# Gate weights and bias through TensorE, another chunk order, split first tile, uneven sums: one change to a fused attention and MLP kernel

## The chip, the cores and the metric

The kernel runs on one core of a Trainium2 chip. The metric is the device time of one execution in microseconds, as the median of several runs. A profile of one execution comes with each kernel. Its "span" goes from the first to the last recorded instruction, so it is about 2 us shorter than the time. Engines are named as in the profile: PE is TensorE's matmuls, PEld its weight loads, DVE is VectorE, ACT is ScalarE, POOL is GpSimd, SP is SyncE, which issues most DMAs (SPq). "L318" is line 318 of the kernel in question. The change shifts line numbers by up to a dozen, so the same instruction has two numbers in the two kernels.

## The reference, cut to what matters

```python
# x: [1, 2048, 448]   16 heads of 28   bf16
q, k, v = split(x @ wqkv)                       # per head
pq, pk  = q @ w_phi, k @ w_phi                  # a 28x28 map per head
phi     = concat(softmax(p), softmax(-p))       # for q and k
kv, z   = sum_s phi_k[s] v[s]^T, sum_s phi_k[s]
o       = (phi_q @ kv) / (phi_q @ z + 1e-6)
a       = o @ wo
b       = gelu(x @ w1 + b1) @ w2 + b2
g       = sigmoid((x * gate_w).sum(-1))
out     = g * a + (1 - g) * b
```

The kernel folds the map into the projections: `Wpk = Wk · map` and `Wpq = Wq · map` are computed once on TensorE (the w_ps products), and then `x @ Wpk` gives `pk` directly. The gate `x · gate_w` is had for nothing as a 449th column of the V or Q projection, and for that the 448 gate weights must stand as a column beside the weights. `b1` must likewise stand as columns, one value per partition, to be the bias of the gelu.

## The kernel before

The order of work in the front part on TensorE is: transposes of the first 512 rows of x (`turn`), V products of the first two units, the Wk map products, K0, the Wq map products, then K1 and V2 (the first V unit with the gate column), and from there a dense run of projections. A unit is two tiles of 128 rows. Cuts are marked by `# ...`.

```python
    nc.gpsimd.dma_start(gb[16:19, :], gate_w[0:384].rearrange("(c p) -> c p", p=P))
    # ... the rest of gate_w and b1 into other rows of gb
    nc.gpsimd.dma_start(b2b[:], B_b2[None, :].to_broadcast([P, D]))

    load_wT(WkT, D)                               # DMA transposes on SP, in this order
    load_wT(WqT, 0)
    load_x(512, 512)
    nc.sync.dma_start_transpose(gbT[:], gb[:])    # rows of gb become columns
    load_x(1024, 512)

    def prep(W_T, W_out, s, copies):              # W_out = W * map, 4 chunks of 128 rows
        for h in (1, 0):
            w_ps = pair("w_ps", slot=(s + 1 - h) % 4)
            for i in range(2):
                c = 2 * h + i
                for m in range(4):
                    # ... one product, 84 to 168 columns
            copies[1 - h](out=W_out[:, 2 * h:2 * h + 2, 0:D], in_=w_ps[:, :, 0:D])

    turn(0, 1, nc.scalar.copy)                    # 4 transposes, one copy
    turn(2, 2, nc.vector.tensor_copy)
    idle(1)                                       # a filler matmul
    v0a = V(0, 3)
    # ... V products
    prep(WkT, Wpk, 1, (nc.scalar.copy, nc.vector.tensor_copy))
    # ... K0
    prep(WqT, Wpq, 3, (nc.vector.tensor_copy, nc.vector.tensor_copy))
    nc.vector.tensor_copy(out=Wpq[:, :, D], in_=gbT[:, 16:20])
    nc.vector.tensor_copy(out=WvG[:, :, D], in_=gbT[:, 16:20])
    nc.vector.tensor_copy(out=b1T[:], in_=gbT[:, 0:NJ])
    # ...
    visit([(K, 1), (V, 2)], [(Q, 0)], 0, 2)
```

PSUM is handled as four slots of two banks each. V2 takes slot 3, the slot in which chunks 2 and 3 of Wpq were summed, so it must wait until these have been copied out. In the middle of the MLP, the eight pairs of heads are summed into kv (`kv_half(0)`, `kv_half(1)`), each half is multiplied by a mask on VectorE, and the first four output tiles are computed from it (`nm` products, then a chain on VectorE that ends in `o_all`).

The softmax here doesn't subtract the row's maximum and nothing guards it: scores larger than these inputs give would overflow.

## Time and profile before

| what | value |
|---|---|
| time, median of 3 runs | 152.53 us (152.49 to 152.59) |
| span of the profiled run | 150.3 us |
| TensorE busy | 144.6 us, 96% of the span |
| VectorE, ACT, POOL busy | 81.7, 63.9, 73.4 us |
| TensorE's longest wait after the start | 1.24 us before V2 |

TensorE is idle for 5.7 us of the span. 3.1 us of that come after its last product, when only the last results have to be added up and stored. The other 2.6 us come before V2 starts, and they are most of what a change that doesn't alter the work can win back. The prediction shows the lines of the chain of waits and of TensorE's timeline.

### The profile page before, as it was taken

What the parts mean: (1) busy time and instruction counts of PE and PEld (TensorE: products, weight loads), DVE (VectorE), ACT (ScalarE), POOL (GpSimd) and SP (SyncE); (2) the same over time, 40 slices, a digit from 0 to 9 for tenths busy, and PEclk for the clock granted to TensorE, in tenths of its full rate; (3) what the DMA queues carried; (4) which work ended last, traced back from release to release, by engine and by line L of the source; (5) the groups of instructions that cost most, each with busy time, mean ns of one, the idle gap of its engine ahead of it and who ended that gap; (6) DMA issues with size and microseconds to landing.
All of it is one profiled execution on the core that took longest, in us unless ns stands there. A gap on an engine that the chain in (4) does not pass through costs nothing.

```text
span 150.3 us, 3083 instructions
## 1 busy us (share of the span) xinstructions
PE 144.6 (96%) x1281; PEld 74.2 (49%) x1281; DVE 81.7 (54%) x139; ACT 63.9 (43%) x71; POOL 73.4 (49%) x60
## 2 busy tenths in 40 slices
PE   7989799999999999999999999999999999999991
PEld 2445344555544444774444445554455555545561
DVE  0248488999969992049995000740637847044112
ACT  3346277989999876506767674000000000000000
POOL 7992127799996999900399960000611110024000
PEclk9999999999999999999999999999999999999999
DMA  4997969679999959994629991140302423303201
GB/s 88 290 196 120 209 153 191 136 170 220 218 219 231 361 126 138 212 120 96 74 41 173 173 139 36 37 100 10 122 31 65 100 70 70 70 2 120 65 31 31
DMA packets 46334, 18.99 MB, mean 126 GB/s; under 512 B 36784, under 2 KB 46128, under 8 KB 46320
## 3 DMA queue, kind: packets, MB, share of 16 engines
q1 hardware_dynamic: 45568, 18.18, 58.3%
q10 hardware_dynamic: 544, 0.37, 0.9%
q0 software_dynamic: 208, 0.23, 0.9%
q8 instruction: 10, 0.16, 0.5%
q14 instruction: 4, 0.03, 0.1%
HBM read 6.34 MB, written 1.84 MB: 54 GB/s over the span
## 4 chain that ended last, share of the span: by engine, by line
PE 88%; DMA 7%; SPq 1%; DVE 1%; issue 0%
PE hp L431 28%; PE y L526 28%; PE y L204 6%; PE q_ps L234 5%; DMA gel<-in_A_wqkv_dram 4%; PE k_ps L234 4%; DMA gbT<-gb 3%; PE v_ps L234 3%; PE nm L455 3%; PE kv L443 2%; PE v_ps L204 2%; PE q_ps L204 2%; PE k_ps L204 2%; PE y L214 1%; PE w_ps L315 1%; SPq L116 1%
## 5 line engine op out<-in xcount | busy, mean ns | idle before, releaser
L526 PE MATMUL y<-w_sb,gel 128*128 128x448 bf16 (+1 forms) x224 | 43.8, 350 | 0.0
L431 PE MATMUL hp<-xT,w_sb 64*128 64x512 bf16 x224 | 42.8, 376 | 0.0
L431 PE MATMUL hp<-xS,w_sb 64*128 64x512 bf16 x168 | 40.7, 376 | 0.0
L435 ACT ACTIVATE gel<-hp,b1T 128x1024 bf16<-128x1024 f32 x28 | 30.8, 1113 | 14.6 <-PE hp L431 14.2
L526 PEld LDWEIGHTS <-gel 128*128 128x128 bf16 x238 | 22.3, 98 | 19.3 <-issue 0.4
L431 PEld LDWEIGHTS <-w_sb 64*128 64x128 bf16 x392 | 18.9, 94 | 23.2 <-DVE o_all L468 0.5
L491 POOL TENSOR_SCALAR b2u<-b2b,ungate 128x448 f32<-128x448 bf16 x16 | 10.0, 637 | 40.5 <-DVE res L538 40.5
L261 POOL TENSOR_TENSOR gel<-gel,rec 128x1792 bf16<-128x1792 bf16 x8 | 25.6, 3212 | 7.1 <-DVE lg L270 4.8
L538 DVE SCALAR_TENSOR_TENSOR res<-y,ungate,b2u 128x448 bf16<-128x448 f32 (+1 forms) x16 | 10.3, 673 | 25.0 <-PE y L526 13.2
L261 POOL TENSOR_TENSOR phiq<-phiq,rec 128x1792 bf16<-128x1792 bf16 x4 | 12.7, 3211 | 9.6 <-DVE rec L260 9.6
L252 ACT ACTIVATE gel<-k_ps 128x896 bf16<-128x896 f32 x16 | 13.7, 922 | 6.5 <-PE k_ps L214 4.9
L258 DVE TENSOR_REDUCE sums<-gel 128x64 f32<-128x1792 bf16 x8 | 16.0, 1996 | 0.0
L462 DVE TENSOR_SCALAR den<-nm,enL 128x16 f32<-128x16 f32 x16 | 3.6, 228 | 17.2 <-PE nm L455 17.2
L261 POOL TENSOR_TENSOR phqT<-phqT,rec 128x1792 bf16<-128x1792 bf16 x4 | 12.7, 3213 | 0.0
L468 DVE TENSOR_TENSOR o_all<-nm,den 128x448 bf16<-128x448 f32 (+2 forms) x24 | 11.0, 485 | 0.6
L234 PEld LDWEIGHTS <-xT 64*128 64x128 bf16 x104 | 8.6, 94 | 4.8
L204 PEld LDWEIGHTS <-xT 128*128 128x128 bf16 x66 | 5.9, 98 | 8.1 <-issue 2.8
L280 DVE CAST vaug<-v_ps 128x896 bf16<-128x896 f32 x7 | 7.5, 1072 | 4.3 <-PE v_ps L214 2.9
L260 DVE RECIPROCAL rec<-sums 128x64 f32<-128x64 f32 x16 | 8.9, 553 | 1.1
L234 PEld LDWEIGHTS <-xS 64*128 64x128 bf16 x78 | 7.3, 94 | 3.6
L234 PE MATMUL q_ps<-gel,xT 64*128 64x448 bf16 x48 | 8.6, 349 | 0.0
L204 PE MATMUL y<-wo_sb,phiq 128*128 128x448 bf16 (+1 forms) x36 | 8.2, 349 | 0.0
(88 smaller groups left out, 149.5 us busy)
## 6 DMA issues: line engine op xcount, KB each, us to landing
w_sb<-in_B_w_dram SPq DMA_DIRECT2D x4, 784.0 KB, 12.3
out_dram<-res SPq DMA_DIRECT2D x15, 112.0 KB, 1.7
w_sb<-in_B_w_dram SPq DMA_DIRECT2D x1, 1568.0 KB, 16.6
xS<-xT SPq DMA_DIRECT2D x8, 96.0 KB, 2.2
phqT<-gel SPq DMA_DIRECT2D x4, 168.0 KB, 3.0
gel<-in_A_x_dram SPq DMA_DIRECT2D x2, 224.0 KB, 4.2
phqT<-gel SPq DMA_DIRECT2D x2, 168.4 KB, 3.2
gel<-in_A_wqkv_dram ACTq DMA_DIRECT2D x1, 336.0 KB, 4.3
```

The costliest lines, as they stand in the source:

```text
L204: nc.tensor.matmul(o, lhsT=self.L(i, slice(0, P), c), rhs=self.R(slice(0, P), c)[:, n0:n1], start=(first and c == 2), stop=(last and c == 1))
L234: nc.tensor.matmul(o, lhsT=tok, rhs=(W if direct else SWAPPED[name])[rows, c, 0:n], start=(k == 0), stop=own)
L252: nc.scalar.activation(out=o, in_=src, func=ACT.Exp, scale=(1.0, -1.0)[s])
L258: nc.vector.reduce_sum(out=sums[:], in_=ph, axis=AX.X)
L260: nc.vector.reciprocal(out=rec[:], in_=sums[:])
L261: eng.tensor_tensor(out=ph, in0=ph, in1=rec[:, :, :, None].to_broadcast([P, 32, 2, DH]), op=ALU.mult)
L431: nc.tensor.matmul(hp[:, i, :].rearrange("p (b t) -> p b t", b=2), lhsT=w1_sb[i * HP:(i + 1) * HP, k, j * P:(j + 1) * P], rhs=x_half(i, k, ...
L435: nc.scalar.activation(out=dst, in_=hp[:].rearrange("p i (b t) -> p i b t", b=2), func=ACT.Gelu_apprx_tanh, bias=b1T[:, j:j + 1])
L468: nc.vector.tensor_tensor(out=o_tok[:, col:col + (b - a) * DH].rearrange("p (q j d) -> p q j d", j=2, d=DH), in0=nm[:, a // 2:b // 2, 0:56 ...
L491: nc.gpsimd.tensor_scalar(out=b2u[t][:], in0=b2b[:], scalar1=ungate[:, place(t):place(t) + 1], scalar2=0.0, op0=ALU.mult, op1=ALU.add)
L526: nc.tensor.matmul(o, lhsT=gel[:, j, tok], rhs=w2_sb[:, j, n0:n1], start=(first and j == 0), stop=(last and j == NJ - 1))
L538: nc.vector.scalar_tensor_tensor(out=res[t][:, n0:n1], in0=o, scalar=ungate[:, e:e + 1], in1=b2u[t][:, n0:n1], op0=ALU.mult, op1=ALU.add)
```

## The change

Its intent: gate and b1 are turned into columns by two matmuls against the identity, with all 128 rows of the array (hence the zeroed 128x128 tiles gb and bb), in place of the DMA transpose. The chunks of the map products are computed in the order 2, 0, 3, 1, and the second Wpq copy goes to ACT. The first tile of x is transposed in two pairs, which VectorE and ACT copy out side by side, and the filler matmul goes. The second load of the map is issued by ACT rather than SP. The sums are cut six pairs and two pairs rather than four and four. The prediction counts these five parts in this order as parts 1 to 5. The broadcast of b2 moves from POOL to the end of SP's loads. The core of the diff, with cuts marked by `...`:

```diff
-    nc.sync.dma_start(wphi[0:HP, 3, :], wflat[384:448, :])
+    nc.scalar.dma_start(wphi[0:HP, 3, :], wflat[384:448, :])
...
-    nc.gpsimd.dma_start(b2b[:], B_b2[None, :].to_broadcast([P, D]))
...
     load_x(512, 512)
-    nc.sync.dma_start_transpose(gbT[:], gb[:])
     load_x(1024, 512)
...
+    def turned_rows(cols, rows):
+        nc.tensor.matmul(cols, lhsT=rows[:], rhs=ident[:, 0:cols.shape[-1]], start=False, stop=True,
+                         skip_group_check=True)
+
+    def prep(W_T, W_out, s, copies, gates=False):
+        w_ps = [pair("w_ps", slot=(s + 1 - h) % 4) for h in (1, 0)][::-1]
+        for c in (2, 0, 3, 1):
...
+            if c == 3 and gates:
+                cols = w_ps[1][:, 1, D:D + 4]
+                turned_rows(cols, gb)
+                for W in (WvG, Wpq):
+                    nc.vector.tensor_copy(out=W[:, :, D], in_=cols)
         for h in (1, 0):
-            copies[1 - h](out=W_out[:, 2 * h:2 * h + 2, 0:D], in_=w_ps[:, :, 0:D])
+            copies[1 - h](out=W_out[:, 2 * h:2 * h + 2, 0:D], in_=w_ps[h][:, :, 0:D])
...
-    turn(0, 1, nc.scalar.copy)
-    turn(2, 2, nc.vector.tensor_copy)
-    idle(1)
+    turn(0, 1, nc.vector.tensor_copy, 2, 4)
+    turn(0, 2, nc.scalar.copy, 0, 2)
+    turn(2, 0, nc.vector.tensor_copy)
...
-    prep(WqT, Wpq, 3, (nc.vector.tensor_copy, nc.vector.tensor_copy))
-    nc.vector.tensor_copy(out=Wpq[:, :, D], in_=gbT[:, 16:20])
-    nc.vector.tensor_copy(out=WvG[:, :, D], in_=gbT[:, 16:20])
-    nc.vector.tensor_copy(out=b1T[:], in_=gbT[:, 0:NJ])
+    prep(WqT, Wpq, 3, (nc.vector.tensor_copy, nc.scalar.copy), True)
...
+    nc.sync.dma_start(b2b[:], B_b2[None, :].to_broadcast([P, D]))
...
+            if kind is V and u == 3:
+                turned_rows(x_.un.ps[:, 1, 460:460 + NJ], bb)
...
-            kv_half(0)
-            kv_half(1)
+            parts = (range(0, 6), range(6, 8))
+            for qs in parts:
+                kv_part(qs)
```

More of the change, by code (lines that the diff above doesn't have):

```diff
@@ L97 @@
     hm = consts.tile([P, 4, 16], BF16, name="hm")
-    gb = consts.tile([32, P], BF16, name="gb")
-    gbT = consts.tile([P, 32], BF16, name="gbT")
+    gb = consts.tile([P, P], BF16, name="gb")
+    bb = consts.tile([P, P], BF16, name="bb")
     b1T = consts.tile([P, NJ], F32, name="b1T")
@@ L113 @@
     nc.vector.memset(gb[:], 0.0)
+    nc.vector.memset(bb[:], 0.0)
     xv = x[0:512, :].rearrange("(j p) d -> p j d", p=P)
@@ L153 @@
                             compare_op=ALU.is_ge, fill=0.0, base=DH - 1, channel_multiplier=-1)
-    nc.gpsimd.dma_start(gb[16:19, :], gate_w[0:384].rearrange("(c p) -> c p", p=P))
-    nc.gpsimd.dma_start(gb[19:20, :].rearrange("o (i p) -> o i p", i=2),
+    nc.gpsimd.dma_start(gb[0:3, :], gate_w[0:384].rearrange("(c p) -> c p", p=P))
+    nc.gpsimd.dma_start(gb[3:4, :].rearrange("o (i p) -> o i p", i=2),
                         gate_w[None, None, 384:448].to_broadcast([1, 2, HP]))
-    nc.gpsimd.dma_start(gb[0:NJ, :], B_b1.rearrange("(j p) -> j p", p=P))
     pk4 = phik.rearrange("p t (q m) -> p (t q) m", m=HP)
@@ L164 @@
     nc.gpsimd.memset(pq4[:, :, 56:64], 0.0)
+    nc.gpsimd.dma_start(bb[0:NJ, :], B_b1.rearrange("(j p) -> j p", p=P))
     nc.gpsimd.memset(o_all[:], 0.0)
@@ L283, in done @@
                 gate(u, t)
+            if u == 3:
+                nc.vector.tensor_copy(out=b1T[:], in_=t[:, 1, 460:460 + NJ])
     class K:
@@ L306, in twin @@
         nc.scalar.copy(out=W_T[:, :, D:512], in_=W_T[:, :, 384:D])
-    def prep(W_T, W_out, s, copies):
-        for h in (1, 0):
-            w_ps = pair("w_ps", slot=(s + 1 - h) % 4)
-            for i in range(2):
-                c = 2 * h + i
-                for m in range(4):
-                    n0, n1 = HEADS[m][0] * DH, HEADS[m][1] * DH
-                    nc.tensor.matmul(w_ps[:, i, n0:n1], lhsT=W_T[:, m, c * P:(c + 1) * P],
-                                     rhs=bd[:, m, 0:n1 - n0], start=(m == 0), stop=(m == 3),
-                                     skip_group_check=True)
-            copies[1 - h](out=W_out[:, 2 * h:2 * h + 2, 0:D], in_=w_ps[:, :, 0:D])
+    def turned_rows(cols, rows):
[4 more added lines that the diff above has]
+        for c in (2, 0, 3, 1):
+            h, i = c // 2, c % 2
+            for m in range(4):
+                n0, n1 = HEADS[m][0] * DH, HEADS[m][1] * DH
+                nc.tensor.matmul(w_ps[h][:, i, n0:n1], lhsT=W_T[:, m, c * P:(c + 1) * P],
+                                 rhs=bd[:, m, 0:n1 - n0], start=(m == 0), stop=(m == 3),
+                                 skip_group_check=True)
+            if c == 3 and gates:
[3 more added lines that the diff above has]
+                    nc.vector.tensor_copy(out=W[:, :, D], in_=cols)
+        for h in (1, 0):
+            copies[1 - h](out=W_out[:, 2 * h:2 * h + 2, 0:D], in_=w_ps[h][:, :, 0:D])
     def idle(n):
@@ L327, with turn @@
     idle(8)
-    def turn(j, slot, copy):
+    def turn(j, slot, copy, c0=0, c1=4):
         tp = pair("tp", BF16, slot)
-        for c in range(4):
+        for c in range(c0, c1):
             dlo = c * P if c < 3 else (384 if j < 2 else 320)
             nc.tensor.transpose(tp[:, 0, c * P:(c + 1) * P], x0[:, j, dlo:dlo + P], ident[:])
-        copy(out=xT[:, :, j * P:(j + 1) * P], in_=tp[:, 0, 0:512].rearrange("p (c t) -> p c t", c=4))
-    turn(0, 1, nc.scalar.copy)
-    turn(2, 2, nc.vector.tensor_copy)
-    idle(1)
+        copy(out=xT[:, c0:c1, j * P:(j + 1) * P],
+             in_=tp[:, 0, c0 * P:c1 * P].rearrange("p (c t) -> p c t", t=P))
+    turn(0, 1, nc.vector.tensor_copy, 2, 4)
+    turn(0, 2, nc.scalar.copy, 0, 2)
+    turn(2, 0, nc.vector.tensor_copy)
     v0a = V(0, 3)
@@ L436, in w1_unit, with kv_part @@
                              func=ACT.Gelu_apprx_tanh, bias=b1T[:, j:j + 1])
-    def kv_half(m):
+    def kv_part(qs):
         kv = pair("kv")[:, 0, :]
-        qs = range(4 * m, 4 * m + 4)
+        n = len(qs)
         for t in range(NT):
-            for q in qs:
-                nc.tensor.matmul(kv[:, (q % 4) * PW:(q % 4 + 1) * PW], lhsT=phik[:, t, q * P:(q + 1) * P],
-                                 rhs=vaug[:, t, q, :], start=(t == 0 and q == qs[0]),
+            for i, q in enumerate(qs):
+                nc.tensor.matmul(kv[:, i * PW:(i + 1) * PW], lhsT=phik[:, t, q * P:(q + 1) * P],
+                                 rhs=vaug[:, t, q, :], start=(t == 0 and i == 0),
                                  stop=(t == NT - 1), skip_group_check=True)
-        nc.vector.tensor_tensor(out=KVbd[:, 4 * m:4 * m + 4, :],
-                                in0=kv[:, 0:4 * PW].rearrange("p (q n) -> p q n", q=4),
-                                in1=mask[:, None, :].to_broadcast([P, 4, PW]), op=ALU.mult)
+        nc.vector.tensor_tensor(out=KVbd[:, qs[0]:qs[0] + n, :],
+                                in0=kv[:, 0:n * PW].rearrange("p (q n) -> p q n", q=n),
+                                in1=mask[:, None, :].to_broadcast([P, n, PW]), op=ALU.mult)
     def o_turned(t):
@@ L495 @@
         if j == 6:
-            kv_half(0)
-            kv_half(1)
+            parts = (range(0, 6), range(6, 8))
+            for qs in parts:
+                kv_part(qs)
             nms = [pair("nm"), pair("nm")]
             nms = [p[:, i, :] for p in nms for i in range(2)]
-            for m in range(2):
+            for qs in parts:
                 for t in range(4):
-                    num_mm(t, nms[t], range(4 * m, 4 * m + 4))
+                    num_mm(t, nms[t], qs)
             for t in range(4):
```

## The prediction

> **What bounds the kernel now.** I read the page first: TensorE is busy for 96% of the span, the granted clock is 0.9 or more in every slice, and the slices that are not full are at the front.
>
> ```profile
> PE 144.6 (96%) x1281; PEld 74.2 (49%) x1281; DVE 81.7 (54%) x139; ACT 63.9 (43%) x71; POOL 73.4 (49%) x60
> ...
> PE   7989799999999999999999999999999999999991
> ```
>
> So the time is TensorE's work plus TensorE's idle time, and a change that leaves the work alone can only win idle time. Second I listed TensorE's own waits, which are short:
>
> ```profile
> PE v_ps L204 <- DVE gel L367: 1.2, 1, 1.2
> PE w_warm L322 <- PEq L587: 0.8, 1, 0.8
> PE w_ps L315 <- DMA gel<-in_A_wqkv_dram: 0.3, 1, 0.3
> ```
>
> Third, the chain of waits in order of time (start us, us, what) says what stands behind the 1.2 us:
>
> ```profile
> 2.94 6.14 DMA gel<-in_A_wqkv_dram
> ...
> 9.13 0.41 PE w_ps L315 x4
> ...
> 9.57 0.88 PE w_ps L315 x12
> ...
> 10.48 0.46 DVE gel L318
> 10.94 4.68 DMA gbT<-gb
> ...
> 15.64 0.18 DVE gel L366
> 15.81 0.08 DVE gel L367
> ...
> 16.03 1.30 PE v_ps L204 x6
> ```
>
> The little transpose of gate and bias through the DMA queue takes 4.68 us from issue to landing; a VectorE copy then puts the gate column into WvG, and the V2 matmuls wait for it. From 16.03 to 61.57 the chain is TensorE alone. The timeline of TensorE (start, us) gives the front step by step:
>
> ```profile
> 4.50 1.03 PE L333 MATMUL tp<-ident,gel 128*128 128x128 bf16 x8
> 5.33 0.59 PE L322 MATMUL w_warm<-const-bfloat16-1.0 128*128 128x512 bf16 x1
> 5.79 0.74 PE L204 MATMUL v_ps<-gel,xT 128*128 128x448 bf16 x3
> 6.36 0.61 PE L333 MATMUL tp<-ident,gel 128*128 128x128 bf16 x8
> ```
>
> The later places with idle time are at the kv sums. In the chain the second half of the nm products begins at 65.81 though the first sixteen, 28.5 ns apart, were issued by 65.62: 0.19 us go on the second mask multiply (VectorE, 65.36 to 65.76). Then the fourth w1 unit after it loads its weights late, at 71.06 ("DVE o_all L468", 0.49 us on the weight loads), which makes the matmuls some 0.16 us late.
>
> **What the Trainium skill says.** (1) "DMA: Bandwidth & Descriptors", section "Issuing engines are not separate DMA queues": starting DMAs on a second engine saves only the sequencer's issue time. The trace has that time: the second map load occupies the SP queue for 0.565 us. (2) Same page, "Anatomy of one DMA — SWDGE (gpsimd) path": a fixed cost of about 2 us, measured on the gpsimd path, mostly the wait for the write receipt. The gbT transpose, issued from SP, has 4.68 us, over twice that; the trace decides. (3) "TensorE: Matmul & The Clock Gate", section "Wait — 56ns, not 53.3ns?": warm matmuls start every N / 2.4 GHz plus about 2.5 ns, so 189 ns for 448 columns; fourteen y matmuls take 2.65 us, 189 ns each, which agrees. (4) "VectorE: DVE Perf Modes", section "The TRN2 errata — SBUF-src ops pay a fixed extra latency per instruction": a copy out of PSUM costs 120 cycles at 0.96 GHz plus its columns. For 896 columns that is 1.06 us, and the trace has 1.09. I use its slope for the sizes that the trace lacks.
>
> **Part 1, gate and b1 by matmul.** It removes the DMA transpose (1.12 us of SP issue, 4.68 us of latency) and three VectorE copies of 0.17 us. It adds one 4-column and one 14-column matmul with 128-column weights, about 0.06 us each (the 84- to 168-column w_ps matmuls run at 0.93 / 16 = 0.058 us: 12.56 to 13.49), and three VectorE copies. The gate column is now made after twelve of the sixteen Wq products, so V2 no longer waits for a DMA. It waits instead for its PSUM slot: V2 takes slot 3, where chunks 2 and 3 of Wpq lie until VectorE has copied them out.
>
> **Part 2, chunk order 2, 0, 3, 1.** Chunk 3 needs the ACT copy of the last columns. Before, the Wk products stop after four (9.13) and go on at 9.57; four at 0.067 us would be 0.27, so about 0.17 us are lost. With chunk 0 in between, nothing is. The price is that ACT's copy of chunks 2 and 3 starts after twelve products, not eight, but the K0 products wait on VectorE's copy of chunks 0 and 1, which comes after all sixteen anyway. One Wpq copy goes to ACT, which in the old trace was idle for 3.18 us just there.
>
> **Part 3, the first x tile in two pairs.** The filler matmul goes and V0 can start after eight transposes, near 5.35: VectorE's 256-column copy should take 0.42 - 0.13 = 0.29 us (estimate, slope as in (4)) from about 4.95, ACT's about 0.4 (the 128x256 copy has 0.41) from 5.14 to 5.55. That would be 0.4 us, but the next transposes need the second x load, and its sixteenth landing event in the trace is at 6.00. Their weight loads began at 6.18, so only about 0.2 us is kept: the V products end at 8.60, not 8.80.
>
> **Part 4, half the map load on ACT.** The Wk transpose is issued 0.6 us earlier (0.56 plus a gap of 0.04). I do not give it all of that. Its packets follow x and the map on the same queue, the DMA share is about 1 from 3.5 to 7.4 us, and the last x packets leave at 5.2. The transposes start moving 2.1 to 2.2 us after issue (2.94 to 5.05, 5.22 to 7.45); an issue at 2.33 would make that 4.5, where the queue is still full. I choose 0.35 us: Wk lands at about 8.75 in place of 9.09.
>
> **The sum for the front** (old time in brackets):
> - Wk products start 8.80 (9.13), sixteen at 0.067 end 9.87 (10.37).
> - VectorE copies chunks 0 and 1 from 9.98 to 11.07 (11.57); K0's second product 11.12 (11.62), five at 0.19, Wq products start 12.06 (12.56). Wq lands at 10.86 already before, so it is not in the way.
> - Sixteen products and the gate one take 0.99: K1 starts 13.05 (13.49), six at 0.19 end 14.19.
> - The gate product is issued at 12.82; VectorE starts 0.2 later, two small copies 0.2, Wpq copy 1.09: 14.30. V2 starts at about 14.40 (16.03).
>
> That is 1.63 us. All DMA of the next stage goes out earlier as well (the SP queue loses the 1.12 us issue with its 0.7 us wait, and 0.6 at the front), and the first w1 half landed at 41.78 for a use at 43.28, so the later stages should move along whole.
>
> **Part 5, uneven sums.** With six pairs first, 24 nm products (0.68 us) cover the second multiply, now 116 columns, about 0.28 us (estimate by the slope in (4) from 0.40 at 232). The 0.19 us hole closes. But the fourth w1 unit waits for VectorE's chain of four output tiles, which starts when tiles 0 and 1 are done: 4 products after the second part's start instead of 8, so this chain moves by only about 0.11. What passes on is 0.11.
>
> Total 1.63 + 0.11 - 0.06 (the b1 matmul) = 1.68: 152.53 - 1.68 = 150.85 us.
>
> **The rivals.** (a) The Wk landing does not move, because the queue is full. For it: the DMA share. Against it: the slow ramp of that transpose, whose packets per quarter us are 135 at 6.0 where 283 are reached later. Then only the chunk order gains in the Wk stage, V2 starts near 14.7 to 14.8 and the time is 151.2. (b) The new wait for the Wpq copy is longer than thought, for instance because VectorE is held by V0's copy or the gate product's release comes late. Each tenth adds a tenth; at half a us, 151.35. The copies are short and the queue order on VectorE is gate, gate, Wpq, so I hold it less likely. (c) A later stage takes the gain back: POOL is busy from 30.07 to 63.26 with one pause of 1.28. But its first task follows the PE chain and the phqT tiles needed at 65.16 land at 61.97, so I see 3 us of room; time 152.3 if it failed. (d) The landings come 0.6 us earlier whole: V2 near 14.2, 150.6.
>
> **Range and chances.** Rivals (a) and (b) together give 151.7, (d) with a fully used hole 150.5; a front in which the x load also lands earlier gives 150.1. Range 150.1 to 151.7. Over 2% faster would need 3.05 us, more than all the TensorE idle time named here. Slower by 2% would need a new wait of 4.7 us.
>
> **What would show it.** Right: no gbT transfer in the chain, V2 at 14.2 to 14.7, its wait ended by the VectorE or ACT copy of w_ps; Wk products without a hole after the fourth; the nm products without the pause; TensorE's busy time unchanged within 0.3. Wrong: V2 waiting on a DMA, the first w1 matmul less than 1.3 us earlier than 43.28, or a new TensorE wait after 16 us.

## More of the kernel before

One view is added here, because it turns out to matter: VectorE's timeline just before V2. The columns are start and duration in us, engine, line, operation, output<-input, shapes, count, and in brackets the idle time before and what ended it.

```profile
13.23 2.09 DVE L318 CAST gel<-w_ps 128x896 bf16<-128x896 f32 x2 [0.66 <-PE w_ps L315]
15.64 0.18 DVE L366 COPY gel<-gbT 128x4 bf16<-128x4 bf16 x1 [0.32 <-DMA gbT<-gb]
```

VectorE copies both halves of Wpq out of PSUM, 2.09 us, until 15.32. Only then is it free for the copy of the gate column, for which it waits another 0.32 us. So two things end close together in front of V2, the transfer and the copies. The chain of waits names only the later of the two.

## The result, and the profile after

The changed kernel takes 150.41 us (median of 4 runs, 150.12 to 150.42), the kernel before 152.51 us in the same rounds (4 runs, 152.34 to 152.59). The ratio is 0.986, with a 95% interval of 0.984 to 0.988. That is within 2%, so it counts as the same, and it lies inside the predicted range of 150.1 to 151.7. All ratios in this document are the mean time of one kernel's fast runs over the mean of the other's in the same rounds, so they are not quite the ratio of the medians quoted. All runs named below gave correct results. One run of the kernel before, of 850 us, was slow and is left out.

The page of the changed kernel, its engine totals and TensorE's busy tenths in 40 slices:

```profile
PE 143.3 (96%) x1282; PEld 73.6 (50%) x1282; DVE 81.0 (54%) x140; ACT 64.6 (43%) x72; POOL 73.0 (49%) x59
...
PE   7889999999999999999999999999999999999991
```

The first line shows busy times within about 1% of those before. The second shows where TensorE's idle time went: the fifth slice (15.0 to 18.8 us in the kernel before, where V2 waits) had a 7 and now has a 9. The chain of waits of the changed kernel, in order of time:

```profile
2.33 6.63 DMA gel<-in_A_wqkv_dram
...
9.01 0.88 PE w_ps L319 x12
...
13.17 0.00 PE w_ps L310
...
14.62 1.30 PE v_ps L203 x6
...
63.86 0.91 PE nm L466 x32
64.77 0.23 DVE den L473
```

No transfer of gate and bias is left in it. The Wk transpose is issued 0.61 us earlier than before (2.33, not 2.94) but takes 6.63 us, not 6.14, so it lands only 0.13 us earlier. The Wk products, of which the chain shows the first twelve, run without the break that they had after the fourth. The gate product (L310) is in the middle of the Wq products and V2 starts at 14.62, not 16.03. The nm products run in one piece of 32. After that, the chain goes through VectorE's work on the first four tiles (from 64.77) and comes back to TensorE only at 69.51, where a w1 unit waited for its last output.

TensorE's own waits, then those of its weight loads (us in total, times, longest):

```profile
PE tp L343 <- DMA gel<-in_A_x_dram: 0.5, 1, 0.5
PE w_ps L319 <- DMA gel<-in_A_wqkv_dram: 0.3, 1, 0.3
PE k_ps L213 <- ACT gel L328: 0.3, 1, 0.3
```

```profile
PEld L442 <- DVE o_all L479: 0.6, 1, 0.6
PEld L203 <- DMA xT<-in_A_x_dram: 0.5, 1, 0.5
```

The wait of 1.2 us for V2 is gone from the first list. In the second, the last line belongs to V2: its weights are put down to the x load. VectorE's timeline shows something that ended later:

```profile
13.24 0.24 DVE L326 CAST gel<-w_ps 128x4 bf16<-128x4 f32 x2 [1.01 <-PE w_ps L310]
13.39 1.08 DVE L328 CAST gel<-w_ps 128x896 bf16<-128x896 f32 x1
```

The x load landed at 14.34. The copy that frees V2's PSUM slot ran from 13.39 to 14.47. V2 started at 14.62. The experiments settle which of the two it was.

Where the time went, in the two profiled runs (us from the start of the span):

| step | before | after | gain |
|---|---|---|---|
| Wk products start | 9.13 | 9.01 | 0.12 |
| V2 starts | 16.03 | 14.62 | 1.41 |
| first w1 product | 43.28 | 41.87 | 1.41 |
| kv products start | 61.51 | 60.10 | 1.41 |
| first y product | 90.81 | 89.25 | 1.56 |
| end of the span | 150.26 | 148.72 | 1.54 |
| time of that run | 152.35 | 150.42 | 1.93 |

Three places carry the gain: 1.41 us before V2, 0.15 us at the kv sums, and 0.39 us that isn't in the span at all. Time less span was 2.09 us before and is 1.70 us after.

### The profile page after: what moved, and what is told of

Its sections match the earlier page's. It is cut to its first block, busy times and chain, and to the rows that moved or that the text cites. A ratio compares the mean times of both kernels' runs of the same rounds, so it can differ in the third digit from the quotient of the medians.

```text
span 148.7 us, 3084 instructions
## 1 busy us (share of the span) xinstructions
PE 143.3 (96%) x1282; PEld 73.6 (50%) x1282; DVE 81.0 (54%) x140; ACT 64.6 (43%) x72; POOL 73.0 (49%) x59
## 4 chain that ended last, share of the span: by engine, by line
PE 88%; DMA 4%; DVE 3%; SPq 1%; ACT 1%; issue 0%
PE y L538 28%; PE hp L442 26%; PE y L203 6%; PE q_ps L233 5%; DMA gel<-in_A_wqkv_dram 4%; PE k_ps L233 4%; PE k_ps L203 3%; PE v_ps L233 3%; PE kv L454 2%; PE nm L466 2%; PE v_ps L203 2%; DVE o_all L479 2%; PE q_ps L203 2%; PE w_ps L319 1%; PE y L213 1%; PE k_ps L213 1%
```

## The experiments

In every trace the same segments have the same length within 0.02 us, whatever the kernel: V2 to the first w1 product 27.25, w1 to kv 18.22, y to the last product 56.16. Only four quantities differ between kernels, and these are what the experiments are read by: the moment at which Wk lands, the stretch from the first Wk product to V2, the stretch from the first kv product to the first y product, and the time less the span.

| kernel | median us (range, runs) | ratio | Wk lands | Wk product to V2 | kv to y | time less span |
|---|---|---|---|---|---|---|
| before | 152.51 (152.34–152.59, 4) | 1 | 9.09 | 6.90 | 29.30 | 2.09 |
| after | 150.41 (150.12–150.42, 4) | 0.986 | 8.96 | 5.61 | 29.16 | 1.70 |
| e1_gate_alone | 150.34 (150.19–151.22, 6) | 0.989 | 8.61 | 5.51 | 29.30 | 1.71 |
| e2_b2b_pool | 150.52 (150.28–150.92, 5) | 0.989 | 8.94 | 5.61 | 29.16 | 1.71 |
| e3_before_b2b_sp | 151.64 (151.54–151.99, 6) | 0.996 | 9.21 | 6.48 | 29.30 | 2.11 |
| e4_map_sp | 150.06 (149.94–150.20, 4) | 0.986 | 8.51 | 5.61 | 29.15 | 1.71 |
| e5_old_turn | 150.92 (150.54–151.15, 4) | 0.990 | 9.31 | 5.61 | 29.16 | 2.09 |
| e9_q_order_old | 150.14 (149.95–150.40, 4) | 0.986 | 8.71 | 5.39 | 29.16 | 1.72 |
| e10_spare_gbt | 150.26 (149.90–150.49, 4) | 0.987 | 8.79 | 5.61 | 29.15 | 1.72 |
| e11_gbt_kept | 150.69 (150.58–151.23, 6) | 0.991 | 8.84 | 5.49 | 29.30 | 2.04 |
| e7_even | 150.57 (150.34–150.65, 4) | 0.988 | 8.99 | 5.61 | 29.29 | 1.71 |
| e12_pair_rec | 150.70 (150.44–150.81, 4) | 0.989 | 9.21 | 5.61 | 28.87 | 2.05 |
| e13_best | 150.45 (150.20–150.65, 5) | 0.988 | 8.90 | 5.39 | 28.87 | 2.05 |
| e14_best_two_spare | 149.88 (149.71–150.23, 5) | 0.985 | 8.74 | 5.39 | 28.87 | 1.73 |

The last four columns come from the profiled run of each kernel. The median of before in the rounds of the experiments was 152.28 to 152.41. A difference of a few tenths between medians of kernels of different rounds says little, because Wk's landing moves by 0.8 us over the table. One and the same kernel moves as much: the spans of e1's six runs go from 148.5 to 149.5 us.

My theory after the result: almost all of the gain is part 1. The rivals were that the front's gain comes from an earlier Wk (parts 3 and 4), or from the chunk order, and for the 0.39 us outside the span that the moved b2 broadcast or the missing transpose causes it.

**e1_gate_alone: part 1 without the other parts.** Edit to the changed kernel: the other parts undone.

```diff
-    nc.scalar.dma_start(wphi[0:HP, 3, :], wflat[384:448, :])
+    nc.sync.dma_start(wphi[0:HP, 3, :], wflat[384:448, :])
...
+    nc.gpsimd.dma_start(b2b[:], B_b2[None, :].to_broadcast([P, D]))
...
-        for c in (2, 0, 3, 1):
+        for c in (2, 3, 0, 1):
...
-    turn(0, 1, nc.vector.tensor_copy, 2, 4)
-    turn(0, 2, nc.scalar.copy, 0, 2)
-    turn(2, 0, nc.vector.tensor_copy)
+    turn(0, 1, nc.scalar.copy)
+    turn(2, 2, nc.vector.tensor_copy)
+    idle(1)
...
-    prep(WqT, Wpq, 3, (nc.vector.tensor_copy, nc.scalar.copy), True)
+    prep(WqT, Wpq, 3, (nc.vector.tensor_copy, nc.vector.tensor_copy), True)
...
-    nc.sync.dma_start(b2b[:], B_b2[None, :].to_broadcast([P, D]))
...
-            parts = (range(0, 6), range(6, 8))
+            parts = (range(0, 4), range(4, 8))
```

> Part 1 alone: gate and b1 by matmul, everything else as before (one x turn and the filler, map on SP, chunk order 2 3 0 1, both Wpq copies on VectorE, even sums, b2b still loaded by POOL). My theory: almost the whole gain of the front belongs to this part. The Wq products start at 12.56 as before, K1 ends near 14.7, the VectorE copy that frees V2's slot ends near 14.5, so V2 starts at 14.7 (16.03 before, 14.62 in the changed kernel) and the span falls by 1.3 us to 149.0. Rival, the sums of the prediction: the other front parts carry 0.5 us, so V2 would start no earlier than 14.9 and the span would be 149.2 or more. On the time outside the span (time minus span: 2.1 us before, 1.7 in the changed kernel): if it belongs to the b2b load it stays at 2.1 here, if to the gbT transpose it falls to 1.7.

Measured: 150.34 us, and 5.51 us from the first Wk product to V2. TensorE's timeline at the end of the front:

```profile
13.04 1.30 PE L204 MATMUL k_ps<-gel,xT 128*128 128x448 bf16 x6
14.17 1.30 PE L204 MATMUL v_ps<-gel,xT 128*128 128x449 bf16 x6
```

K1 (13.04) runs straight into V2 (14.17). With part 1 alone the front is 1.39 us shorter than before, and 0.10 us shorter than with all parts together. Set against the 0.14 us that the uneven sums bring, the other four parts add 0.04 us to part 1 in what can be measured apart from Wk's landing. (Part 1 also brings VectorE to 140 instructions, which matters further down.) So the theory holds, and the other parts need a closer look.

**e2_b2b_pool and e3_before_b2b_sp: the b2 broadcast moved.** In e2 the changed kernel issues it on POOL again; in e3 the kernel before issues it at the end of SP's loads.

```diff
# e2, against the changed kernel (e3 is the reverse edit of the kernel before)
+    nc.gpsimd.dma_start(b2b[:], B_b2[None, :].to_broadcast([P, D]))
...
-    nc.sync.dma_start(b2b[:], B_b2[None, :].to_broadcast([P, D]))
```

> The changed kernel with the b2 load back on POOL's queue. Theory: the 0.4 us that the result has beyond the span (152.35 - 150.3 = 2.1 before, 150.42 - 148.7 = 1.7 after) come from having one POOL load less, so the span stays at 148.7 and the time goes up to about 150.8. Rival: it has nothing to do with that load; time 150.4.

> The kernel before with only the b2 load moved from POOL to the end of the SP loads. Theory of the POOL load: span 150.3 as before, time 0.4 us lower, 152.1. Rival: nothing moves, 152.5.

Measured: e2 is the changed kernel in every column. e3 keeps the 2.11 us outside the span, so the broadcast isn't what that depends on, and my theory is refuted by both. The time of e3, 151.64 us, lies below both times that I had named. But e3 holds a surprise: the small transpose of gate and bias, issued at 11.1, lands after 2.3 us rather than 4.7, at 13.3 rather than 15.61. The DMA line in the view of that tile, in e3:

```profile
DMA to landing us min/median/max: 2.3/2.3/2.3
```

In the kernel before, POOL issues the 112 KB broadcast half a us after this transpose. The view of its tile there:

```profile
L174 POOL DMA_DIRECT2D b2b<-in_B_b_dram x1: 588/588/588, 11.4 to 11.4; - x1
DMA to landing us min/median/max: 3.9/3.9/3.9
```

So the broadcast lands at about 15.3, and the transpose then lands at 15.61. The Trainium skill has a rule that fits, in "DMA: Bandwidth & Descriptors", section "Queues, rings and completion order": the increment of the semaphore lands only after every earlier write of that DMA engine, across its queues. The two runs in which the broadcast was moved (e3 and e11) show that it costs the transpose 2.4 us there. That the order of writes is how it does so is not shown. A rival is that the transpose's packets wait their turn between those of the broadcast. The packet records of the kept traces (no view prints them) leave both open: 32 four-byte packets of SP's queue, which I take for the transpose's signals, go out from 13.27 to 14.84 us among the broadcast's data packets, and from 12.83 to 12.98 us in e3. Yet V2 gained only 0.42 us from the earlier landing, and VectorE's timeline in e3 says why:

```profile
13.35 2.09 DVE L317 CAST gel<-w_ps 128x896 bf16<-128x896 f32 x2 [0.66 <-PE w_ps L314]
15.36 0.17 DVE L365 COPY gel<-gbT 128x4 bf16<-128x4 bf16 x1
```

The column is there at 13.3, but its copy stands in VectorE's queue behind both copies of Wpq. The wait that the change removes had two layers, and taking away the first one alone leaves the second. (The copy on ACT alone was not run. The transfer would then still land at about 15.6, so it can hardly help by itself.)

**e11_gbt_kept: both layers removed, but the DMA transpose kept.** Edit to the kernel before: e3's edit, and the second Wpq copy on ACT.

```diff
-    nc.gpsimd.dma_start(b2b[:], B_b2[None, :].to_broadcast([P, D]))
...
-    prep(WqT, Wpq, 3, (nc.vector.tensor_copy, nc.vector.tensor_copy))
+    prep(WqT, Wpq, 3, (nc.vector.tensor_copy, nc.scalar.copy))
...
+    nc.sync.dma_start(b2b[:], B_b2[None, :].to_broadcast([P, D]))
```

> The kernel before with the gbT transpose kept, the b2 load moved to the end of the SP loads and the second Wpq copy given to ACT. In the run with the b2 load moved alone gbT landed at 13.3 and V2 still waited until 15.74, for the two Wpq copies that stand ahead of the column copies on VectorE. Theory: the DMA transpose was not what cost the time by itself; V2 now starts near 14.7 to 14.9, 5.6 us after the first Wk product as in the changed kernel, and the span is 148.8 to 149.0. Time minus span stays at 2.1, so the time is near 151.0. Rival: the transpose is on the path in any case; V2 not before 15.5, time 151.6 as without the ACT copy.

Measured: 5.49 us from the first Wk product to V2, as short as with the matmul. VectorE's timeline:

```profile
12.98 1.09 DVE L317 CAST gel<-w_ps 128x896 bf16<-128x896 f32 x1 [0.66 <-PE w_ps L314]
13.98 0.17 DVE L365 COPY gel<-gbT 128x4 bf16<-128x4 bf16 x1
```

The column copies now come after one Wpq copy, at 13.98 and 14.05, and V2 starts at 14.37, right after K1. So the DMA transpose as such wasn't what V2 lost its time to. A transfer that collided with it and a queue order on VectorE were. The matmuls cure both at once, but a moved line and a copy on another engine do the same for the front.

**e4_map_sp and e5_old_turn: parts 4 and 3 undone.** Edits to the changed kernel:

```diff
# e4
-    nc.scalar.dma_start(wphi[0:HP, 3, :], wflat[384:448, :])
+    nc.sync.dma_start(wphi[0:HP, 3, :], wflat[384:448, :])
```

```diff
# e5
-    turn(0, 1, nc.vector.tensor_copy, 2, 4)
-    turn(0, 2, nc.scalar.copy, 0, 2)
-    turn(2, 0, nc.vector.tensor_copy)
+    turn(0, 1, nc.scalar.copy)
+    turn(2, 2, nc.vector.tensor_copy)
+    idle(1)
```

> The changed kernel with both map loads on the SP queue. Theory: the Wk transpose is held by the full DMA queue and not by its issue, so Wk lands at 9.0 to 9.1 against 8.96, and V2, which waits for an x landing and a copy, starts within 0.1 us of 14.62: time 150.4 to 150.5. Rival: the issue time counts in full, Wk lands 0.6 us later and the time is 150.9 to 151.0.

> The changed kernel with the first x tile turned whole again and the filler matmul back. My theory: in the traces so far Wk lands 0.1 to 0.4 us after the V products are done, at any time from 8.5 to 9.2 whatever the kernel, so the turn is hidden: V2 starts 5.61 us after the first Wk product as in the changed kernel, the distance from the last V product to the first Wk product shrinks, time 150.1 to 150.5. Rival, the prediction: the two pairs are worth 0.2 us, and the Wk products start 0.2 us later relative to the Wk landing; time 150.6.

Measured: in e4, with the map on SP again, Wk landed at 8.51, the earliest of all kernels, where I had expected 9.0 to 9.1, and the time of 150.06 us is below my 150.4 to 150.5. In e5 it landed at 9.31, the latest. Neither changes the stretch from the Wk product to V2. In both the last V product begins about half a us before Wk comes (8.03 in e4, 8.80 in e5), and in all 14 traces the first Wk product starts 0.04 or 0.05 us after the landing. So the form of the x transposes is not what holds the Wk products up. Nothing in the table ties Wk's landing to where the map is issued: with it on SP the landings are 9.09, 8.61, 9.21, 8.51 and 8.84, with it on ACT (the nine others) 8.71 to 9.31. Part of the scatter is already in the landing of x: the first x transposes start anywhere from 4.24 (e14) to 4.85 us (e5). But measured from that start, Wk lands after 4.42 us on average with the map on SP and 4.43 us with it on ACT. The issue times of the transposes (SP's own timeline, Wk and Wq together), in the kernel before and then after:

```profile
2.94 4.56 SPq L125 DMA_TRANSPOSE gel<-in_A_wqkv_dram  x2
```

```profile
2.33 5.32 SPq L126 DMA_TRANSPOSE gel<-in_A_wqkv_dram  x2
```

The issue starts 0.61 us earlier and takes 0.76 us longer. What is saved at the start is lost within the issue itself. It is so over all traces: the x transpose, next in SP's queue, is issued at 7.42 to 7.63 us in the five kernels with the map on SP and at 7.33 to 7.85 us in the nine with it on ACT. The packets show the same for Wk: the first packet of its transpose moves at 5.20 us in both profiled runs (5.17 to 5.43 in all), though it was issued at 2.94 and at 2.33, and the last packet of the first x loads starts at 5.28 and 5.43 us. That fits a queue that is still full of x, as the prediction's rival (a) has it. No experiment took x away, so it is not shown. My expectation for e5's time was missed (150.92 us, too slow). Of that, 0.39 us are outside the span again, and the rest goes with the late landing.

**e9_q_order_old: the old chunk order for Wq alone.** Edit to the changed kernel:

```diff
-    def prep(W_T, W_out, s, copies, gates=False):
+    def prep(W_T, W_out, s, copies, gates=False, order=(2, 0, 3, 1)):
...
-        for c in (2, 0, 3, 1):
+        for c in order:
...
-    prep(WqT, Wpq, 3, (nc.vector.tensor_copy, nc.scalar.copy), True)
+    prep(WqT, Wpq, 3, (nc.vector.tensor_copy, nc.scalar.copy), True, (2, 3, 0, 1))
```

> The changed kernel with chunk order 2 3 0 1 for Wq alone (the ACT copy of its last columns is done long before there). Theory: what V2 waits for in the changed kernel is VectorE's copy out of its PSUM slot and not the x landing; the gate product and that copy come 0.23 us earlier (four products of 0.058), the V2 products follow K1 with no gap (0.41 us between two starts before, 0.19 now), and V2 starts 5.39 us after the first Wk product: time 0.2 us below the changed kernel's. Rival: V2 waits for the x transpose, which lands as before; the gap stays.

Measured: 5.39 us, 0.22 us less than the changed kernel, and 150.14 us. TensorE's timeline:

```profile
13.02 1.30 PE L203 MATMUL k_ps<-gel,xT 128*128 128x448 bf16 x6
14.15 1.30 PE L203 MATMUL v_ps<-gel,xT 128*128 128x449 bf16 x6
```

V2 (14.15) follows K1 (13.02, six products of 0.19) without a hole. With chunks 2 and 3 first, the gate product comes after eight map products rather than twelve (at 12.53 here), VectorE starts its copies four products earlier, and the slot is free in time. This settles what V2 waits for in the changed kernel. The gap from K1's last product to V2 is 0.40 to 0.41 us in all seven kernels of the table that have the new order for Wq, while the x load landed in these anywhere from 13.48 to 14.34 us. It is the copy out of the PSUM slot, and the profile's "DMA xT" was the wrong one of two. For Wk the new order pays: the Wq products begin 3.31 us after the first Wk product, before 3.43.

**e7_even: even sums.** Edit to the changed kernel:

```diff
-            parts = (range(0, 6), range(6, 8))
+            parts = (range(0, 4), range(4, 8))
```

> The changed kernel with even sums (four pairs and four) again. Theory: the second mask multiply is seen again by 0.19 us among the nm products, the wait of the fourth w1 unit behind them is 0.1 us shorter, so from the first kv product to the first y product it takes 29.30 us as in the kernel before (29.15 in the changed one): time 0.15 us more. Rival: the fourth unit's wait swallows all of it, and the distance stays at 29.15.

Measured: kv to y is 29.29 us, 0.13 more than with uneven sums. So part 5 is worth what it seemed, 0.13 to 0.14 us.

**e12_pair_rec: a shorter chain on VectorE after the sums.** The chain of the changed kernel still goes through four output tiles on VectorE. Here the reciprocal is taken for two tiles in one instruction (the new helper `num_pair` is left out here, and the comment is not in the run's code).

```diff
-            for t in range(4):
-                num_out(t, nms[t])
+            num_pair(0, nms[0:2])     # two den, one reciprocal, then the o_all of both
+            num_pair(2, nms[2:4])
```

> The changed kernel with one reciprocal for two output tiles in the first four tiles (VectorE alone). Theory: the stretch from kv to y is now bound by VectorE's chain of four tiles; two reciprocals of 0.25 us fewer end that chain 0.4 us earlier, the gap before the fourth w1 unit (0.49 us between two starts where 0.22 is usual) closes, and kv to y takes 28.88 us: time 0.27 us less. Rival: another slot wait takes its place; no gain.

Measured: kv to y is 28.87 us, 0.29 less. The chain of waits now stays on TensorE:

```profile
64.11 0.90 PE nm L466 x32
65.01 24.28 PE hp L442 x224
```

The time is nevertheless 150.70 us, not the 0.27 us less that I expected: in the profiled run Wk landed late (9.21), and in every run 2.0 to 2.1 us lie outside the span.

**e10_spare_gbt: what lies outside the span.** The changed kernel with an unused transpose of gb at the end of SP's loads, to ask whether having this transpose lengthens the part outside.

```diff
+    gbT = consts.tile([P, 32], BF16, name="gbT")
...
+    nc.sync.dma_start_transpose(gbT[:], gb[0:32, :])
```

> The changed kernel with a spare DMA transpose of gb into a tile that nobody reads, issued behind all the loads. Theory: the 0.4 us outside the span (time minus span 2.1 us in the kernels that have this transpose, 1.7 in those that have not) belong to it wherever it stands; span 148.2 to 148.8, time minus span 2.1. Rival: they belong to something else in part 1 (the small tiles, the VectorE copies), and time minus span stays at 1.7.

Measured: 1.72 us outside the span, as without it, so this theory is refuted too. The transpose is not the cause either; e5, which has none, has 2.09. What does go with it over all the kernels is a number on the page, the count of VectorE's instructions: the eight kernels with 140 (after, e1, e2, e4, e7, e9, e10, e14) have 1.7 to 1.8 us outside the span in each of their runs, the six with 138 or 139 have 2.0 to 2.1 us in each of theirs.

**e13_best and e14_best_two_spare: the best of the parts, and the test of that count.** e13 is e9 and e12 together. It has 138 VectorE instructions on the page. e14 adds two that do nothing of use at the very start:

```diff
     nc.vector.memset(warm[:], 0.0)
+    nc.vector.memset(warm[:], 0.0)
+    nc.vector.memset(warm[:], 0.0)
```

> The changed kernel with the old chunk order for Wq and the shared reciprocals together. If both theories hold, the gains add: 0.5 us below the changed kernel of the same rounds' level, about 149.7, ratio to the kernel before near 0.983. Rival: the earlier V2 runs into the x transpose landing, which leaves 0.3 us.

> The combination of the last job (old chunk order for Wq, shared reciprocals) with two spare VectorE memsets of a two-element tile at the very start, where VectorE is idle for 3 us. In the thirteen traces so far the time outside the span is 1.70 to 1.72 us where VectorE has 185 records in the trace, and 2.04 to 2.11 us where it has 183 or 184, whatever else differs; this kernel has 185. Theory: the time outside the span goes with VectorE's number of instructions, so every run here has time minus span 1.7, the span stays at 148.2 to 148.6 as without the memsets, and the time is 150.1 (150.45 without them). Rival: the association is chance, and time minus span stays at 2.05.

Measured: e13 150.45 us with 2.05 us outside the span, e14 149.88 us with 1.68 to 1.73 in all five runs. In e13 the two shorter stretches add up as expected (5.39 and 28.87 us), but the expected time of 149.7 was missed because of the part outside. Two idle instructions more made the part outside the span 0.3 us shorter, as the count foretold. This shows by intervention that the count, or something that two more instructions shift, matters. It is not the number of all instructions in the trace: e5 has 3085 and 2.09 us, the changed kernel 3084 and 1.70 us. Why is open. Only counts of 138 to 140 were tried, and the position of the extra ones only at the start. e14 has the lowest median of all, with a ratio of 0.985 to the kernel before (0.983 to 0.986). That overlaps the changed kernel's 0.984 to 0.988, and the two didn't share rounds, so the times alone don't show that e14 is faster than the changed kernel. Its trace gives the cleaner comparison: 0.22 us less before V2 and 0.29 us less at the sums.

## Why the prediction was right or wrong

The time (150.85 predicted, 150.41 measured) and the class were right. By its own steps:

- **What bounds the kernel**: right, the gain is idle time, most of it taken away at the front. TensorE's busy time fell by 1.3 us (144.6 to 143.3), which is not the "unchanged within 0.3" foretold. But this sum scatters: e2, the changed kernel with one load moved and equally without the filler matmul (0.59 us), has 144.3. Of the 1.3 us, 0.75 lie before the first Wk product, where e2 has 1.0 us more than the changed kernel. The stretches of dense work are as long as before.
- **Part 1**: right in size. The prediction has V2 5.60 us after the first Wk product (14.40 less 8.80); measured 5.61, before 6.90. A little luck is in the match: Wq's products came 0.05 us later after Wk's than summed (3.31, not 3.26), and V2 0.03 us sooner after these (2.31, not 2.34). "It waits instead for its PSUM slot" is right too, as e9 shows. Its reading of the cause was too short, though: "the V2 matmuls wait for it" names the transfer only. VectorE's queue was the second layer (e3), and the transfer was slow because of a neighbour (e3, e11), not because it is a transfer.
- **Part 2**: "With chunk 0 in between, nothing is [lost]" is right for the Wk products, worth 0.12 us at the start of the Wq products. "The K0 products wait on VectorE's copy of chunks 0 and 1" is half right. K0's first two products now waited 0.28 us for ACT's copy of chunks 2 and 3, which starts 0.9 us after the first Wk product in both kernels (10.01 before, 9.91 after); so the time saved in the Wk products is lost again here. The gain comes from VectorE's copy, which is done 2.22 us after the first Wk product rather than 2.44: K0's products from 11.17 on follow each other at 0.2 us, without the break of 0.35 us before (11.27 to 11.62). What the prediction didn't weigh is that for Wq the same order puts the gate product and the copy four products later, which costs 0.22 us (e9). Over the whole front the order is a loss.
- **Part 3**: its 0.2 us was not in the sum and indeed can't be seen. V's last product starts at 8.32, before 8.45, and TensorE then waits for Wk in both.
- **Part 4**: this is the term of the sum that was mis-sized. "I choose 0.35 us" became 0.13 in the two profiled runs, and as e4 has the earliest landing without part 4, even that can't be credited to it. Rival (a), "the Wk landing does not move, because the queue is full", was right that nothing comes of it; that the full queue is the reason fits the packets but is not shown. One reading behind the estimate is off: "5.22 to 7.45" is not in the kept trace, which has the Wq transpose issued at 5.86, so that 7.45 is 1.6 us later, not 2.2. The delay from issue to first movement was not a constant that could be carried over to an earlier issue: for Wk it was 2.26 us before and 2.87 us after. The estimate treated a landing that wanders by 0.8 us from kernel to kernel as a fixed time. V2's gain of 1.41 instead of 1.63 is this one term, 0.21 us, with 0.01 for the rest.
- **Part 5**: 0.11 predicted, 0.14 measured (0.13 by e7). The estimated 0.28 us for the 116-column multiply was what the trace shows. (So was the 0.29 us for the 256-column copy in part 3. It took off 0.13 us for 256 columns, though, which is half of what the slope quoted in (4) gives, 0.27 us.) The chain of four tiles was the limit that remained, as said; e12 confirms it by taking it away.
- **The b1 matmul**: 0.06 us was subtracted, nothing shows. V2 to the first w1 product is 27.25 us before and 27.26 after.
- **Rival (c)**, that a later stage takes the gain back, fell: 1.41 us at V2 is 1.41 at w1 and at kv.
- **What was not foreseen**: 0.39 us outside the span. The prediction worked within the span and took the rest as constant. Within the span the gain was 1.54 us in place of 1.68; the 0.39 us came on top by luck. That is nearly all of the 0.44 us by which the result beats 150.85. Without it the time would have been about 150.8, still in the range.

## What to carry to other kernels

Where a wait is named after one transfer, look at what the waiting engine's queue does at that moment: here moving a neighbour's DMA and one copy does as much as replacing the transfer. Judge parts by stretches that repeat from trace to trace (first product to first product), and don't let a jittering landing decide on a gain of a few tenths. When a new order of products helps one use of a helper, try it for each use apart; it was a gain for Wk and a loss for Wq.

## What the Trainium skill lacked or had wrong

- "DMA: Bandwidth & Descriptors", section "Anatomy of one DMA — SWDGE (gpsimd) path": the fixed cost of about 2 us is near the 2.3 us that the small transpose from SP took in e3, but it took 4.7 with a 112 KB broadcast of POOL in flight. The section has no such case. The section "Queues, rings and completion order" of the same page has a rule that may explain it, without a number for what it costs.
- "Advanced Engine Details and Errata", section "X-Bar Transpose (TRN2)", says that transposes are as fast as regular DMAs. No run here moved the same data both ways, so this is open; the large Wk transpose took 6.1 to 6.6 us from issue to landing in the two profiled runs, with x and the map ahead of it.
- No page says how far a landing wanders. The same Wk transpose landed between 8.51 and 9.31 us over the 14 kernels, with no relation to the changes made that could be seen.
- "DMA: Bandwidth & Descriptors", section "Issuing engines are not separate DMA queues": it says that a second issuing engine saves only the issue time. Here even that was not kept: the issue of the next two transposes began 0.61 us earlier and took 0.76 us longer in the two profiled runs, and over the 14 traces the transpose after them was issued no earlier.
- No page says that the time outside the profiled span depends on the program: 2.0 to 2.1 us with 138 or 139 VectorE instructions on the page, 1.7 to 1.8 us with 140, and two spare memsets switch it.
